# Pooled attention and a SiLU MLP on one core: q cast in its transfer, token parity on row halves, weights in full-partition loads, the first token tile in two column parts

## The chip, the core and the metric

The program runs on one NeuronCore of a Trainium2 chip. The core has TensorE (matmuls; "PE" in the profile, "PEld" for its weight loads), VectorE ("DVE"), ScalarE ("ACT"), GpSimd ("POOL") and SyncE ("SP"). Each engine works through its own instructions in order and waits on semaphores for others. Transfers between HBM and the on-chip memory SBUF are issued from SP's queue, POOL's queue or ACT's queue and run on 16 shared DMA engines; a transfer that changes the type (float32 to bf16) is issued from POOL here. Matmul results go to PSUM banks, from which VectorE and ScalarE copy them.

The metric is the time of one execution on the device in microseconds (us), the median of several runs.

## The reference

Keys and values are averaged over groups of 8 tokens, so each head attends from 576 queries to 72 pooled keys. The result, put back into token order, goes through a two-layer MLP with SiLU. All inputs and the output are float32.

```python
B, H, S, D = q.shape                                  # 8, 8, 576, 64
k_p = k.reshape(B, H, S // 8, 8, D).mean(axis=3)
v_p = v.reshape(B, H, S // 8, 8, D).mean(axis=3)
scores = (1 / np.sqrt(D)) * np.matmul(q, k_p.transpose(0, 1, 3, 2))
attn = np.exp(scores - scores.max(-1, keepdims=True))
attn = attn / (attn.sum(-1, keepdims=True) + 1e-09)
o = np.matmul(attn, v_p)                              # B, H, S, D
x = o.transpose(0, 2, 1, 3).reshape(B * S, H * D)     # 4608 x 512
h = x @ w_in                                          # 512 x 2048
out = (h * (1 / (1 + np.exp(-h)))) @ w_out            # 2048 x 512
```

## The kernel before

The 4608 tokens are 8 batches of 576 for the attention and 9 token tiles of 512 for the MLP. The attention of batch 0 stands ahead of everything. Then, for tile t, `up` (L299) makes 16 hidden groups of 128 features with 4 matmuls of 512 columns each, and ScalarE applies SiLU to each (L306); `down` (L319) makes 4 output blocks of 128 tokens with 16 matmuls each, VectorE copies a block out (L326) and SP stores it in two transfers of 64 rows (L329). While tile t runs, the attention of batch t+1 is woven in between its matmuls: `spread` takes a list of (step, work) pairs and issues each work item when the matmul count reaches its step. All instructions are placed by hand in this way (`manual_schedule`): an engine runs them in the order in which the code issues them.

Names that the prediction speaks of:

- `q_raw` (L98) is a batch of q in float32, loaded by two transfers of 64 partitions on SP's queue. POOL casts it to `q_bf` in four instructions (L109), TensorE transposes it to `qT_ps` in two groups of five and two of four (L121), VectorE copies to `qT` (L127). A token's number inside the batch is p * 9 + i; `qT` holds the tokens in the order (i, p), and the stores undo that order.
- K and V of batches 0 and 1 come "flat" (`load_kv_flat`, L182): K on partitions 0 to 63 and V on 64 to 127 of `kv_raw`. VectorE sums groups of 8 in a tree of additions (L145, L149), doubles the result (L196), TensorE transposes it (L206), and K goes to `kz`, V to `vT`, which is transposed back to `vp` (L226, L227). From batch 2 on, K and V come on 72 partitions each (`load_kv`, L137), are summed by the same tree, and K is transposed in four pieces (L165) and copied to `kz` (L173).
- `kz[n]` holds the keys of a pair of heads so that one half of the 128 rows is zero: a score matmul (L235) takes the 128 rows of two heads' queries and the key weights of one of them.
- `scores` makes two heads' scores for 288 tokens, with an exponential on ScalarE (`es`, L242). `values` makes the denominators (`den_ps`, L252), the numerators (`nu_ps`, L260), the reciprocal by a logarithm and an exponential on ScalarE (L268, L270) and the products into `xT` (L272). One pair of `scores` and one `values` is called a visit; a batch has four.
- `w_in_sb` is loaded by 16 casting transfers of 32 partitions on POOL's queue (L351), `w_out_sb` by 4 of 128 partitions behind them (L361). POOL's queue has eight completion semaphores: the ninth transfer is issued when the first has landed. POOL's casts of batch 1's q stand behind all of these.

Of the kernel before, what the change touches and what calls it, by code (L numbers as in the profile page):

```python
# [36 lines left out]
def kernel(  # L37
# [17 lines left out]
    NP = H // 2  # L55
# [3 lines left out]
    NT = NTOK // NTT  # L59

    QI = S // 64
    QC = (5, 4)

    KI = H * SP // 64
    S8 = 64 // H
    HS = S // 2
    score_scale = float(1.0 / (D ** 0.5) / POOL)
    assert NT == B + 1 and NP == KF and H == 8 and sum(QC) == QI == KI

    w_out_r = moe_w_out.rearrange("(kt kp) d -> kp kt d", kp=128)  # L70

    w_in_r = moe_w_in.rearrange("(g hh c dd) f -> hh c dd g f", g=2, hh=4, c=2)
    out_r = out.rearrange("(b p i) d -> b i p d", p=64, i=QI)

    singles = ctx.enter_context(tc.tile_pool(name="singles", bufs=1))
    big = ctx.enter_context(tc.tile_pool(name="big", bufs=2))
    mid = ctx.enter_context(tc.tile_pool(name="mid", bufs=2))
    psum = ctx.enter_context(
        tc.tile_pool(name="psum", bufs=1, space=bass.MemoryType.PSUM)
    )  # L80
    ctx.enter_context(tc.manual_schedule())


    ident = singles.tile([128, 128], BF16, name="ident")
    ones = singles.tile([SP, 32], BF16, name="ones")
    w_in_sb = singles.tile([128, KF, d_ff], BF16, name="w_in_sb")
# [3 lines left out]
    kz = [singles.tile([128, H, SP], BF16, name=f"kz{n}") for n in range(2)]  # L90
# [3 lines left out]
    def load_q(b):  # L94
        st = batches.setdefault(b, {})
        q_raw = big.tile([128, H // 2, QI * D], FP32, tag="q_raw", name="q_raw")
        for g in range(2):
# [4 lines left out]
        st["q_raw"] = q_raw  # L102

    def cast_q(b):
        st = batches[b]
        q_bf = big.tile([128, 2, QI, 2, D], BF16, tag="q_bf", bufs=1, name="q_bf")
        for a in range(2):
            for s in range(2):
                nc.gpsimd.tensor_copy(  # L109
                    out=q_bf[:, a, :, s, :],  # L110
                    in_=st["q_raw"][:, 2 * a + s, :].rearrange("q (i d) -> q i d", d=D),
                )
        st["q_bf"] = q_bf
        st["qT"] = mid.tile([128, NP, S], BF16, tag="qT", bufs=1, name="qT")

    def q_transpose(b, a, c):
        st = batches[b]
        i0, n = (0, QC[0]) if c == 0 else (QC[0], QC[1])
        qT_ps = psum.tile([128, n, 128], BF16, tag="nd", bufs=3, name="qT_ps")
        for i in range(n):  # L120
            nc.tensor.transpose(  # L121
                qT_ps[:, i, :],
                st["q_bf"][:, a, i0 + i, :, :].rearrange("q s d -> q (s d)"),
                ident,
            )
        dst = st["qT"].rearrange("d (g a) (i p) -> d a i g p", g=2, p=64)
        nc.vector.tensor_copy(  # L127
            out=dst[:, a, i0 : i0 + n],
            in_=qT_ps.rearrange("d i (g p) -> d i g p", g=2),
        )  # L130


    def load_kv(b):
        st = batches.setdefault(b, {})
        for name, src in (("k", k), ("v", v)):
            raw = big.tile([SP, H, POOL * D], FP32, tag=f"{name}_raw", bufs=1, name="raw")
            nc.sync.dma_start(  # L137
                out=raw, in_=src[b].rearrange("h (sp p) d -> sp h (p d)", p=POOL)
            )
            st[f"{name}_raw"] = raw  # L140

    def tree(dst, raw):
        w = POOL * D // 2
        while w > D:
            nc.vector.tensor_add(  # L145
                out=raw[:, :, :w], in0=raw[:, :, :w], in1=raw[:, :, w : 2 * w]
            )
            w //= 2
        nc.vector.tensor_add(out=dst, in0=raw[:, :, :D], in1=raw[:, :, D : 2 * D])  # L149

    def pool_k(b):
        st = batches[b]
        st["kp"] = mid.tile([SP, H, D], BF16, tag="kp", bufs=1, name="kp")
        tree(st["kp"], st["k_raw"])

    def pool_v(b):
        st = batches[b]
        st["vp"] = mid.tile([SP, H, D], BF16, tag="vp", name="vp")
        tree(st["vp"], st["v_raw"])

    def k_transpose(b):
        st = batches[b]
        kT_ps = psum.tile([128, NP, SP], BF16, tag="nd", bufs=3, name="kT_ps")
        for p in range(NP):
            nc.tensor.transpose(  # L165
                kT_ps[:, p, :],
                st["kp"][:, 2 * p : 2 * p + 2, :].rearrange("s h d -> s (h d)"),
                ident[:SP, :SP],
            )
        dst = kz[b % 2].rearrange("d (p s) k -> d s p k", s=2)  # L170
        for s in range(2):
            rows = slice(s * D, (s + 1) * D)
            nc.vector.tensor_copy(out=dst[rows, s], in_=kT_ps[rows])  # L173


    def load_kv_flat(b, parts):
        st = batches.setdefault(b, {})
        raw = big.tile([128, KI, POOL * D], FP32, tag="kv_raw", bufs=1, name="kv_raw")
        for i in range(parts):
            ii = slice(i * KI // parts, (i + 1) * KI // parts)  # L180
            for half, src in ((0, k), (64, v)):
                nc.sync.dma_start(  # L182
# [253 lines left out]
```

## Time and profile before

| | us |
|---|---|
| median of 3 runs | 351.69 |
| lowest and highest run | 351.60 and 650.59 |
| the profiled execution | 351.98 |
| its span in the profile | 350.2 |

The profiled execution is the one that all lines below come from; 1.8 us of it lie outside the span. In a line of the chain of waits stand the start, the length and what ran. In a line of the timeline stand start, length, engine, line of the code, operation, what it writes and reads, shape, count, and in brackets the idle time before it with what ended it. In a group line stand the busy time, the mean of one in ns, the idle time before such instructions and what ended it. In the windows stand the stretch, its length, the busy time (and count) of PE, PEld, DVE, ACT and POOL, the granted clock of TensorE, the mean busy share of the DMA engines and what they moved in GB/s. In the table of transfers stand the issuing queue, the count, the size of one as it lands in SBUF, and the median time to landing.

### The profile page before, as it was taken

To read this page: it belongs to the slowest core of one execution; us is meant where nothing else is said; L and a number is where in the kernel's file an instruction comes from. 1 tells how busy PE (TensorE), PEld (TensorE's weight loads), DVE (VectorE), ACT (ScalarE), POOL (GpSimd) and SP (SyncE) were. 2 spreads that over 40 slices of the span, in tenths; PEclk is the share of its full clock that TensorE was granted. 3 is DMA by queue.
4 is the path that set the end of the run, shared out by engine and by line. 5 is a ranking of instruction groups with operands and counts; after the bars stand their busy time and mean duration, and the time that the engine had idled before them with its cause. 6 is when DMAs were issued, how large, how long until landed. Compare 5 with 4: busy or idle time off the path is not lost.

```text
span 350.2 us, 4636 instructions
## 1 busy us (share of the span) xinstructions
PE 308.6 (88%) x1858; PEld 146.0 (42%) x1858; DVE 137.3 (39%) x204; ACT 177.3 (51%) x299; POOL 50.3 (14%) x61
## 2 busy tenths in 40 slices
PE   0336878499999999999999999999999999999994
PEld 0212334144544454445444544454445444444441
DVE  0641651033653456365546553754376231020011
ACT  1026628045675566555755665566566656604600
POOL 2731232000060006000500240033000000000000
PEclk9999989679999999999999999999999999999999
DMA  7999999612866296628653964496420021022022
GB/s 170 223 249 238 238 239 216 121 32 62 176 142 153 59 204 135 154 61 194 138 137 72 204 143 110 93 198 140 96 60 0 21 63 40 0 60 63 0 55 65
DMA packets 21221, 42.24 MB, mean 121 GB/s; under 512 B 2000, under 2 KB 4048, under 8 KB 21072
## 3 DMA queue, kind: packets, MB, share of 16 engines
q1 hardware_dynamic: 17808, 37.76, 47.2%
q0 software_dynamic: 3392, 4.20, 6.8%
q8 instruction: 14, 0.23, 0.3%
q14 instruction: 7, 0.06, 0.1%
HBM read 36.70 MB, written 9.44 MB: 132 GB/s over the span
## 4 chain that ended last, share of the span: by engine, by line
PE 74%; DMA 17%; ACT 4%; POOL 1%; issue 1%; SPq 0%; DVE 0%; POOLq 0%
PE o_ps L319 33%; PE hp_ps L299 32%; DMA w_in_sb<-in_moe_w_in_dram 8%; DMA w_out_sb<-in_moe_w_out_dram 7%; PE sc_ps L235 4%; ACT L277 2%; DMA q_raw<-in_q_dram 2%; PE nu_ps L260 2%; PE den_ps L252 2%; PE qT_ps L121 2%; ACT es L242 1%; ACT h_T L306 1%; POOL q_bf L109 1%; POOL w_out_sb L361 0%; PE kT_ps L165 0%
## 5 line engine op out<-in xcount | busy, mean ns | idle before, releaser
L319 PE MATMUL o_ps<-w_out_sb,h_T 128*128 128x512 bf16 x576 | 142.9, 385 | 6.1 <-DMA w_out_sb<-in_moe_w_out_dram 6.1
L299 PE MATMUL hp_ps<-xT,w_in_sb 128*128 128x512 bf16 x576 | 134.5, 385 | 0.0
L306 ACT ACTIVATE h_T<-hp_ps 128x512 bf16<-128x512 f32 x144 | 85.8, 597 | 70.5 <-PE hp_ps L299 70.4
L319 PEld LDWEIGHTS <-h_T 128*128 128x128 bf16 x576 | 56.2, 99 | 67.4 <-issue 15.8
L299 PEld LDWEIGHTS <-w_in_sb 128*128 128x128 bf16 x576 | 55.4, 99 | 61.6 <-issue 3.9
L272 DVE TENSOR_TENSOR xT<-nu_ps,rec 128x288 bf16<-128x288 f32 x64 | 26.3, 453 | 98.8 <-ACT rec L270 87.5
L109 POOL CAST q_bf<-q_raw 128x576 bf16<-128x576 f32 x32 | 37.0, 1196 | 167.0 <-PE qT_ps L121 118.6
L242 ACT ACTIVATE es<-sc_ps 72x576 bf16<-72x576 f32 x64 | 41.4, 647 | 28.4 <-PE sc_ps L235 28.2
L326 DVE COPY o_sb<-o_ps 128x512 f32<-128x512 f32 x36 | 24.8, 690 | 62.4 <-PE o_ps L319 62.4
L145 DVE TENSOR_TENSOR raw<-raw 72x2048 f32<-72x2048 f32 (+1 forms) x24 | 44.8, 1868 | 0.4
L235 PE MATMUL sc_ps<-qT,kz 128*72 128x288 bf16 x128 | 28.5, 307 | 7.7 <-ACT es L242 7.7
L268 ACT ACTIVATE lnd<-den_ps 128x288 f32<-128x288 f32 x32 | 13.1, 410 | 31.8 <-PE den_ps L252 31.8
L127 DVE COPY qT<-qT_ps 128x640 bf16<-128x640 bf16 (+1 forms) x32 | 14.5, 458 | 35.1 <-PE qT_ps L121 35.1
L121 PE MATMUL qT_ps<-ident,q_bf 128*128 128x128 bf16 x144 | 14.1, 233 | 12.8 <-POOL q_bf L109 12.7
L235 PEld LDWEIGHTS <-kz 128*72 128x72 bf16 x128 | 15.4, 122 | 21.5 <-issue 12.3
L121 PEld LDWEIGHTS <-q_bf 128*128 128x128 bf16 x144 | 11.2, 105 | 20.0 <-POOL q_bf L109 13.6
L260 PE MATMUL nu_ps<-es,vp 72*32 72x288 bf16 x256 | 14.8, 311 | 0.5 <-ACT lnd L268 0.5
L270 ACT ACTIVATE rec<-lnd 128x288 f32<-128x288 f32 x32 | 14.2, 445 | 1.0
L219 ACT COPY vT<-kvT_ps 64x160 bf16<-64x160 bf16 (+1 forms) x8 | 2.2, 274 | 21.5 <-DVE kz L216 21.3
L280 ACT ACT_TABLE_LOAD x9 | 11.5, 1283 | 0.2
L277 ACT ACT_TABLE_LOAD x8 | 10.3, 1283 | 0.9 <-PEq L420 0.7
L351 POOL DMA_DIRECT2D w_in_sb<-in_moe_w_in_dram x16 | 8.6, 544 | 13.8 <-DMA w_in_sb<-in_moe_w_in_dram 13.8
(26 smaller groups left out, 65.5 us busy)
## 6 DMA issues: line engine op xcount, KB each, us to landing
q_raw<-in_q_dram SPq DMA_DIRECT2D x16, 576.0 KB, 7.4
out_dram<-o_sb SPq DMA_DIRECT2D x72, 128.0 KB, 2.3
raw<-in_k_dram SPq DMA_DIRECT2D x6, 1152.0 KB
raw<-in_v_dram SPq DMA_DIRECT2D x6, 1152.0 KB
w_in_sb<-in_moe_w_in_dram POOLq DMA_DIRECT2D x16, 128.0 KB, 16.7
w_out_sb<-in_moe_w_out_dram POOLq DMA_DIRECT2D x4, 512.0 KB, 22.9
kv_raw<-in_k_dram SPq DMA_DIRECT2D x3, 384.0 KB, 10.6
kv_raw<-in_v_dram SPq DMA_DIRECT2D x3, 384.0 KB, 11.7
```

The source lines that it names most:

```text
L109: nc.gpsimd.tensor_copy(out=q_bf[:, a, :, s, :], in_=st["q_raw"][:, 2 * a + s, :].rearrange("q (i d) -> q i d", d=D),)
L121: nc.tensor.transpose(qT_ps[:, i, :], st["q_bf"][:, a, i0 + i, :, :].rearrange("q s d -> q (s d)"), ident,)
L145: nc.vector.tensor_add(out=raw[:, :, :w], in0=raw[:, :, :w], in1=raw[:, :, w : 2 * w])
L235: nc.tensor.matmul(sc_ps[:, s, :HS], lhsT=kz[b % 2][:, 2 * p + s, :], rhs=st["qT"][:, p, cols], start=True, stop=True,)
L242: nc.scalar.activation(es, sc_ps[:, :, :HS], func=AF.Exp, scale=score_scale)
L260: nc.tensor.matmul(nu_ps[32 * hh : 32 * (hh + 1), :HS], lhsT=st["vp"][:, 4 * g + hh, 32 * c : 32 * (c + 1)], rhs=es[hh // 2][:, hh % 2, :] ...
L272: nc.vector.tensor_mul(out=xT[:, 2 * g + c, cols], in0=nu[c][:, :HS], in1=rec)
L277: nc.scalar.preload_act_table_set("natural_log_exp_and_others")
L299: nc.tensor.matmul(hp_ps, lhsT=w_in_sb[:, kk, g * 128 : (g + 1) * 128], rhs=xT[:, kk, t * NTT : (t + 1) * NTT], start=(kk == 0), stop=(kk ...
L306: nc.scalar.activation(h, hp_ps, func=AF.Silu)
L319: nc.tensor.matmul(o_ps, lhsT=h_T[g][:, m * 128 : (m + 1) * 128], rhs=w_out_sb[:, g, :], start=(g == 0), stop=(g == KG - 1),)
L326: nc.vector.tensor_copy(out=o_sb, in_=o_ps)
```

## The change

The tokens of a batch are dealt differently. A token's number is now p * 18 + i with 32 values of p. q's transfer goes from POOL's queue and casts to bf16 on the way, with one row of 18 tokens per (head, p) on 128 partitions and two halves; `q_raw` and POOL's casts are gone. A transpose of 128 columns takes two neighbouring tokens (even and odd i), so `qT` holds the even tokens on rows 0 to 63 and the odd ones on rows 64 to 127. `kz[n]` gets a copy for each parity, with the other half of the rows zero; for this the pooled K is written twice (`kp` with a dimension of 2), transposed in 8 pieces instead of 4 and copied 64 x 576 instead of 64 x 288. The flat way of K and V is gone: all batches use 72 partitions, batch 0 in two halves of four heads each. The numerators take every second column of `vp`.

`w_in` comes in six transfers of 128 partitions (two rows of `w_in` per partition). q of batch 1 is issued between `w_in` and `w_out`, q of the later batches behind `w_out`. In batch 0 the order of the work is new, ScalarE copies `qT`, the last two visits take their reciprocal on VectorE, and eight matmuls on zeros stand at the head of TensorE's queue. PSUM is shared out differently for batch 0 (two score buffers, four of the others).

In tile 0, `up` runs all 16 groups on the first 288 columns and then on the other 224, with the work of batch 1 woven into the second part; `down` makes blocks 0 to 2 side by side, hidden group by hidden group, and then block 3. In the last tile the last block is made in two halves of 256 columns; the second half is copied by ScalarE and VectorE. A block is stored in four transfers of 32 rows.

```diff
-    def load_q(b):
+    def load_q(b, parts=1):
...
-            nc.sync.dma_start(
-                out=q_raw[64 * g : 64 * (g + 1), :, :],
-                in_=q[b, 4 * g : 4 * (g + 1)].rearrange("h (p i) d -> p h (i d)", i=QI),
-            )
...
-                nc.gpsimd.tensor_copy(
-                    out=q_bf[:, a, :, s, :],
-                    in_=st["q_raw"][:, 2 * a + s, :].rearrange("q (i d) -> q i d", d=D),
-                )
+            nc.gpsimd.dma_start(
+                out=q_bf[:, i * n : (i + 1) * n, :], in_=q_r[b][:, i * n : (i + 1) * n, :]
+            )
...
+    def load_one(b, name, parts=1):
...
+            nc.sync.dma_start(out=raw[:, hs, :], in_=src[:, hs, :])
...
+        tree([st["kp"][:, hs, u, :] for u in range(2)], st["k_raw"][:, hs, :])
...
-                lhsT=kz[b % 2][:, 2 * p + s, :],
-                rhs=st["qT"][:, p, cols],
+                lhsT=kz[b % 2][:, f, 2 * pr + u, :],
+                rhs=st["qT"][:, 2 * pr + u, :],
...
-                    lhsT=st["vp"][:, 4 * g + hh, 32 * c : 32 * (c + 1)],
+                    lhsT=st["vp"][:, 4 * g + hh, c::2],
...
+        if on_dve:
+            nc.vector.reciprocal(rec, den_ps[:, :HS])
...
+        for n in parts:
+            for g in range(KG):
...
+                    nc.tensor.matmul(
+                        hp_ps[:, :n],
+                        lhsT=w_in_sb[:, kk, g * 128 : (g + 1) * 128],
+                        rhs=xT[:, kk, t * NTT + n0 : t * NTT + n0 + n],
...
+            for cs in [slice(0, 256), slice(256, 512)] if final else [slice(0, 512)]:
+                for g in range(KG):
+                    for m, ps in zip(mm, o_ps):
...
+                    if cs.start:
+                        nc.scalar.copy(o_sb[:64, cs], ps[:64, cs])
+                        nc.vector.tensor_copy(out=o_sb[64:, cs], in_=ps[64:, cs])
...
-                nc.gpsimd.dma_start(
-                    out=w_in_sb[32 * hh : 32 * (hh + 1), c32::2, cs],
-                    in_=w_in_r[hh, c32][:, :, cs],
-                )
+        for c0, c1 in ((0, 512), (512, 1024), (1024, 2048)):
+            for g in range(2):
+                nc.gpsimd.dma_start(
+                    out=w_in_sb[:, 2 * g : 2 * g + 2, c0:c1], in_=w_in_r[g][:, :, c0:c1]
+                )
+        load_q(1)
...
+        h_T = up(t, f_up, (HS, NTT - HS) if t == 0 else (NTT,))
+        down(
+            t, h_T, f_down,
+            [(0, 1, 2), (3,)] if t == 0 else [(m,) for m in range(NTT // 128)],
+            last=t == NT - 1,
+        )
```

How the order of instructions moves is shown at three places. POOL's instructions from the start on, before (a row has the line, the operation, what it writes and reads, its shape and the count):

```order
L109 CAST q_bf<-q_raw 128x9x64 x4
L351 DMA w_in_sb<-in_moe_w_in_dram 32x2x1024 x16
L361 DMA w_out_sb<-in_moe_w_out_dram 128x4x512 x4
L109 CAST q_bf<-q_raw 128x9x64 x28
```

And now:

```order
L105 DMA q_bf<-in_q_dram 128x1152 x2
masks.py:197 MEMSET ident 128x128
masks.py:199 ISA
masks.py:199 AFFINE_SELECT ident<-ident 128x128
L324 DMA w_in_sb<-in_moe_w_in_dram 128x2x512 x4
L324 DMA w_in_sb<-in_moe_w_in_dram 128x2x1024 x2
L105 DMA q_bf<-in_q_dram 128x2x1152
L330 DMA w_out_sb<-in_moe_w_out_dram 128x4x512 x4
L105 DMA q_bf<-in_q_dram 128x2x1152 x6
```

POOL's queue now begins with q of batch 0 and has q of batch 1 ahead of `w_out`; the casts are gone. SP's queue, before, up to the stores of tile 0:

```order
L98 DMA q_raw<-in_q_dram 64x4x576 x2
L182 DMA kv_raw<-in_k_dram 64x1536
L182 DMA kv_raw<-in_v_dram 64x1536
L182 DMA kv_raw<-in_k_dram 64x1536
L182 DMA kv_raw<-in_v_dram 64x1536
L182 DMA kv_raw<-in_k_dram 64x1536
L182 DMA kv_raw<-in_v_dram 64x1536
L98 DMA q_raw<-in_q_dram 64x4x576 x2
L182 DMA kv_raw<-in_k_dram 64x4608
L182 DMA kv_raw<-in_v_dram 64x4608
L98 DMA q_raw<-in_q_dram 64x4x576 x2
L137 DMA raw<-in_k_dram 72x8x512
```

And now:

```order
L134 DMA raw<-in_k_dram 72x4x512 x2
L134 DMA raw<-in_v_dram 72x4x512 x2
L134 DMA raw<-in_k_dram 72x8x512
L134 DMA raw<-in_v_dram 72x8x512
L134 DMA raw<-in_k_dram 72x8x512
L134 DMA raw<-in_v_dram 72x8x512
L272 DMA out_dram<-o_sb 32x512 x16
```

SP's queue has only K and V ahead of the stores, and each load from the third on waits until VectorE has summed the batch before it out of the same buffer. TensorE's queue where `down` of tile 0 begins, before (the numbers tell tiles of one name apart: `o_ps_500` is the first output block, each `h_T` a hidden group, `kz1_75` the keys of batch 1):

```order
L319 LDWEIGHTS h_T_336
L319 MATMUL o_ps_500<-w_out_sb_72,h_T_336 128x512
L319 LDWEIGHTS h_T_343
L319 MATMUL o_ps_500<-w_out_sb_72,h_T_343 128x512
L235 LDWEIGHTS kz1_75
L235 MATMUL sc_ps_504<-qT_327,kz1_75 72x288
```

And now (`o_ps_564`, `565` and `566` are the blocks 0, 1 and 2):

```order
L288 LDWEIGHTS h_T_304
L288 MATMUL o_ps_564<-w_out_sb_70,h_T_304 128x512
L288 LDWEIGHTS h_T_304
L288 MATMUL o_ps_565<-w_out_sb_70,h_T_304 128x512
L288 LDWEIGHTS h_T_304
L288 MATMUL o_ps_566<-w_out_sb_70,h_T_304 128x512
```

Where one block walked through all hidden groups, and so through all of `w_out`, three blocks now take the same hidden group one after the other.

More of the change, by code (lines that the diff above doesn't have):

```diff
@@ L54 @@
     d_ff = moe_w_in.shape[1]
-    NP = H // 2
     KF = d_model // 128
@@ L168, in k_transpose @@
                 ident[:SP, :SP],
             )
[L170 to L182, printed above, removed]
-                    out=raw[half : half + 64, ii, :],
-                    in_=src[b].rearrange(
-                        "h (s i p) d -> (h s) i (p d)", s=S8, i=KI
-                    )[:, ii, :],
-                )
-        st["kv_raw"] = raw
```

350 lines of the change are left out of this document (166 added, 184 removed).

## The prediction

> **What bounds the kernel now.** I read the page's first block, then the chain of waits in order of time, then the windows of the DMA engines. First the page: span and TensorE.
>
> ```profile
> span 350.2 us, 4636 instructions
> PE 308.6 (88%) x1858; PEld 146.0 (42%) x1858; DVE 137.3 (39%) x204; ACT 177.3 (51%) x299; POOL 50.3 (14%) x61
> ```
>
> TensorE is busy 88% of the span, so at most 41.6 us could go without less matmul work. The chain (start, length, what) says where the rest sits.
>
> ```profile
> 1.57 7.26 DMA q_raw<-in_q_dram
> ...
> 12.08 9.61 DMA w_in_sb<-in_moe_w_in_dram
> ...
> 21.97 18.17 DMA w_in_sb<-in_moe_w_in_dram
> ...
> 43.73 25.22 DMA w_out_sb<-in_moe_w_out_dram
> ...
> 86.73 4.53 PE hp_ps L299 x21
> ...
> 120.64 4.53 PE hp_ps L299 x21
> ...
> 154.55 4.53 PE hp_ps L299 x21
> ```
>
> From 1.57 to 68.95 us (43.73 + 25.22) the chain is transfers almost alone. From 86.73 it is TensorE, and one token tile follows the other at 33.91 us (120.64 - 86.73 and 154.55 - 120.64). So the kernel has two stages: a start that waits for bytes up to 68.95, then 17.78 us of tile 0, then eight tiles bound by TensorE. The change can win in the first stage; in the second it can only add or remove TensorE work.
>
> How fast bytes come is read from the windows (stretch, its length, busy time of five engines, clock, DMA share, GB/s), and how many from the page's table of issues.
>
> ```profile
> 0.00:2.00 2.00, 0.00 (x0) 0.00 (x0) 0.00 (x0) 1.26 (x1) 1.39 (x9) 1.00 0.00 0
> ...
> 8.00:16.00 8.00, 2.78 (x21) 1.99 (x21) 3.81 (x9) 0.00 (x0) 6.81 (x12) 1.00 1.02 224
> 131.00:136.00 5.00, 5.00 (x29) 2.42 (x27) 4.43 (x3) 3.36 (x6) 4.38 (x3) 1.00 0.81 172
> ...
> 46.00:56.00 10.00, 10.00 (x60) 5.13 (x58) 3.58 (x8) 4.83 (x10) 2.71 (x5) 0.83 1.16 237
> 57.00:64.00 7.00, 4.05 (x23) 2.04 (x22) 0.00 (x0) 4.88 (x8) 0.00 (x0) 1.00 0.86 198
> q_raw<-in_q_dram SPq DMA_DIRECT2D x16, 576.0 KB, 7.4
> raw<-in_k_dram SPq DMA_DIRECT2D x6, 1152.0 KB
> w_in_sb<-in_moe_w_in_dram POOLq DMA_DIRECT2D x16, 128.0 KB, 16.7
> w_out_sb<-in_moe_w_out_dram POOLq DMA_DIRECT2D x4, 512.0 KB, 22.9
> ```
>
> Where transfers of both queues run, the share is 0.86 to 1.16: the DMA engines are full, and what counts is bytes. The table counts what lands: a q batch is two issues (1152 KB in float32), a K or V batch 1152 KB, the weights 16 x 128 + 4 x 512 = 4096 KB in bf16. Ahead of the last weights before go q of three batches, K and V of three, and the weights: 3456 + 6912 + 4096 = 14464 KB = 14.81 MB. Nothing moves in the first 2.0 us; from there to 68.95 it is 221 GB/s, between the rows' 198 and 237. The sum of bytes explains the landing.
>
> Two rows bound the kinds. Two 64-row halves side by side go at 224 GB/s (8 to 16 us); one 72-row K or V load alone goes at 172 (131 to 136 us).
>
> **The change part by part: the last weights.** q lands as bf16, so a batch costs 576 KB. q of batch 2 moves behind the weights in POOL's queue. Ahead of the last w_out piece then lie K and V of batches 0 to 2 (6912 KB), q of batches 0 and 1 (1152 KB) and the weights (4096 KB): 12160 KB = 12.45 MB. K of batch 2 is issued as soon as VectorE has summed K of batch 1, and V of batch 2 behind q's transposes of batch 1, whose q lies ahead of w_out; so I count both. At 221 GB/s this is 56.3 us, and the last piece lands at 58.3. The bounds: 12.45 MB at the slow mixed row of 198 gives 64.9; without V of batch 2 (11.27 MB) at 237 gives 49.6. I take the middle one, as it is the average that explained the landing before.
>
> [...]
>
> **Tile 0 behind the last weights.** Before, `down` finished one 128-token row block after the other, so all but a few of its 64 matmuls stood behind the last piece. Now three blocks go side by side, group by group.
>
> ```profile
> 60.96 1.02 PE L319 MATMUL o_ps<-w_out_sb,h_T 128*128 128x512 bf16 x4 [1.18 <-DMA w_out_sb<-in_moe_w_out_dram]
> ...
> 66.79 1.87 PE L319 MATMUL o_ps<-w_out_sb,h_T 128*128 128x512 bf16 x4 [4.56 <-DMA w_out_sb<-in_moe_w_out_dram]
> ...
> 173.78 0.31 PE L252 MATMUL den_ps<-es,ones 72*32 72x288 bf16 x4
> 173.91 0.42 PE L260 MATMUL nu_ps<-es,vp 72*32 72x288 bf16 x8
> 174.26 0.39 PE L319 MATMUL o_ps<-w_out_sb,h_T 128*128 128x512 bf16 x1
> 174.49 0.41 PE L235 MATMUL sc_ps<-qT,kz 128*72 128x288 bf16 x2
> 174.74 1.46 PE L319 MATMUL o_ps<-w_out_sb,h_T 128*128 128x512 bf16 x6
> ...
> L326 DVE COPY o_sb<-o_ps 128x512 f32<-128x512 f32 x36 | 24.8, 690 | 62.4 <-PE o_ps L319 62.4
> ```
>
> Behind the last piece stand 12 matmuls of the three blocks, 16 of the fourth, and of the attention of batch 1 two value groups and two score pairs. A warm matmul is 4.53/21 = 0.216 us (the row at 86.73). After a wait of 4.56 us four took 1.87 us, 0.47 each; after 1.18 us four took 1.02. The twelve follow a wait between these: half of them slow at 0.43, half at 0.216, 3.9 us (bounds 2.6 and 5.2). The fourth block reuses a bank of the first three, so TensorE waits for one VectorE copy (690 ns, the last row) and its semaphores, 1.0 us in all. Then 16 x 0.216 = 3.45, and by the starts above 2 x 0.48 + 2 x 0.25 = 1.46. Sum 9.8, against 17.78 before. Tile 1 starts at 58.3 + 9.8 = 68.1; that is 18.6 us earlier.
>
> [...]
>
> **What hides behind that.** The start of batch 0 is chained through VectorE and the K/V loads.
>
> ```profile
> 37.19 6.19 PE L299 MATMUL hp_ps<-xT,w_in_sb 128*128 128x512 bf16 x21
> L145 DVE TENSOR_TENSOR raw<-raw 72x2048 f32<-72x2048 f32 x12 | 28.4, 2370 | 0.0
> L145 DVE TENSOR_TENSOR raw<-raw 72x1024 f32<-72x1024 f32 x12 | 16.4, 1366 | 0.4
> L149 DVE TENSOR_TENSOR vp<-raw 72x512 bf16<-72x512 f32 x6 | 5.9, 976 | 0.2
> L149 DVE TENSOR_TENSOR kp<-raw 72x512 bf16<-72x512 f32 x6 | 4.1, 687 | 0.2
> 160.28 0.29 PE L165 MATMUL kT_ps<-ident,kp 72*128 72x72 bf16 x4
> 160.41 0.81 PE L299 MATMUL hp_ps<-xT,w_in_sb 128*128 128x512 bf16 x3
> ...
> PE qT_ps L121 <- POOL q_bf L109: 12.7, 2, 10.3
> ```
>
> K and V of batch 0 are 2304 KB = 2.36 MB: alone at 172 GB/s they land at 15.7 us, with half of the 237 GB/s at 21.9; I take 20. Half a V tree is (2.37 + 1.37 + 0.98)/2 = 2.4 us, and about 4 us of values, reciprocals and products follow: `up` starts near 27 instead of 37.19. w_in behind q of batch 0 (2.69 MB at half of 237) lands near 25, so it is no later than that. `up` is 64 x 0.216 = 13.8 us in two parts (the columns are the same, 288 + 224), about 3 us more for a slow clock at its start, and 1.3 us of transposes (18 of q, 8 of K); `down` with four attention visits is 13.8 + 4 x 0.98, and 1.0 for the copy. This ends at 63.8, 4.3 us ahead of 68.1: it is the cover of all startup edits (copies on ScalarE, split K and V, two reciprocals on VectorE), and the floor if the weights come sooner. TensorE waited for a POOL cast twice, in batch 0 and in tile 0 (the last row), and both waits end before the weights come: taking all 32 casts out is worth nothing more.
>
> **The steady tiles and the end.** K of a batch needs 8 transposes instead of 4: four took 0.13 us (160.28 to 160.41), so 0.13 more in six tiles, 0.8. K's last addition is done twice (0.69 more on VectorE), which ends about when TensorE reaches the transposes: 0 to 0.2 us a tile, taken as 0.5 in all. The 32-row stores double SP's issues, behind which only stores and the next K and V stand; nothing. The strided `vp` weights: nothing, as loads run ahead of matmuls (the rival below has the price). Steady: +1.3, bounds 0 and 2.5.
>
> ```profile
> 339.67 5.78 PE L319 MATMUL o_ps<-w_out_sb,h_T 128*128 128x512 bf16 x26
> ...
> 345.48 0.69 DVE L326 COPY o_sb<-o_ps 128x512 f32<-128x512 f32 x1 [2.76 <-PE o_ps L319]
> L260 PEld LDWEIGHTS <-vp 72*32 72x32 bf16 x256 | 7.1, 101 | 1.6 <-issue 0.8
> ```
>
> At the end the last copy is half as wide and shared by two engines, 0.69 to about 0.35: -0.3 (bounds -0.7 and +0.3, as four stores follow in place of two).
>
> **Sum.** 350.2 - 18.6 + 1.3 - 0.3 = 332.6 us of span. The profiled run took 351.98, 1.8 more than its span: 334.4 us. It was 0.3 above the median of 351.69, which I leave inside the range.
>
> **The rivals.** First: the weights land before the floor, and tile 1 starts at 63.8, 22.9 us earlier: 330. For it: casting loads that use all rows share the engines evenly at 46 to 56 us, where 237 GB/s flowed. Against it: K and V in 72 rows.
>
> Second: the engines run at the slow row throughout, the last piece lands at 64.9, tile 1 starts at 74.7: 12.0 us won, 341.0. For it: the row at 57 to 64 us is just this mix. [...]
>
> Third: the change doesn't bring the weights sooner. They land at 68.95 as now, because q now stands ahead of them in their own queue and the 72-row loads eat the saved bytes; only the side-by-side `down` stays. Tile 1 at 78.8, 8.0 us won: 345.0, within 2%. Against it: 2.36 MB fewer bytes.
>
> Fourth, on the other side: the strided `vp` weights (every second column) are no longer loaded ahead. Their row has 256 loads at 101 ns. Exposed in full they cost 25.9 us, 360.3 in all. It decides from 24.3/256 = 95 ns a load. Against it: eight matmuls with their loads now start within 0.35 us (173.91 to 174.26).
>
> **How the numbers follow.** The forecast has 0.50, its own range 331 to 338; the first rival 0.18, the second 0.18, the third 0.10, the fourth 0.04. About 2% is what a measurement can tell from no change, here 344.7 and 358.7. Faster: 0.50 + 0.18 + 0.16 of the second = 0.84; same: 0.02 + 0.10 = 0.12; slower 0.04. The range 328 to 343 leaves out the third and fourth (0.14) and 0.06 of the tails of the others.
>
> **What would show it.** The wait of `down` for w_out should end near 58 and tile 1's first `up` matmul stand near 68, with tiles 33.9 to 34.2 apart. `up` of tile 0 should begin near 27. If the period grows by more than 0.4 us, the strided loads or K's second addition cost; if the last w_out wait ends past 66, bytes were not saved or share badly; if no wait for w_out is left, tile 0 is bound by TensorE and the first rival holds.

## The result and the profile after

The changed kernel takes 331.53 us (median of 4 runs, 331.24 to 331.74) against 351.64 for the kernel before on the same chip: a ratio of 0.944, with a 95% interval of 0.9411 to 0.947. It is faster, inside the range, 2.9 us below the forecast of 334.4. Ratios leave out runs over 1.5% above the fastest of the same kernel: here one of 650.59 us of the kernel before, and below two of the four of `kv64` (338.75 and 339.07 us, beside 333.29 and 334.50). The profiled execution took 331.45 us, with a span of 329.7, against 350.2 before: 20.5 us less.

The head of the page (span, busy time, share, instructions):

```profile
span 329.7 us, 4895 instructions
PE 307.2 (93%) x1960; PEld 154.3 (47%) x1960; DVE 146.8 (45%) x216; ACT 177.6 (54%) x306; POOL 14.2 (4%) x25
```

TensorE is as busy as before (307.2 and 308.6 us), so what went is idle time: 41.6 us of it before, 22.5 now. The chain of waits up to tile 2 (start, length, what) says where it went and what bounds the start now:

```profile
1.24 8.57 DMA q_bf<-in_q_dram
9.85 1.14 PE qT_ps L116 x9
...
17.84 0.43 DVE vp L145
...
23.15 1.88 DVE rec L216
25.11 0.82 DVE xT L222 x2
25.94 1.88 DVE rec L216
27.91 0.83 DVE xT L222 x2
28.78 12.68 PE hp_ps L254 x85
...
65.84 4.53 PE hp_ps L254 x21
...
99.88 4.53 PE hp_ps L254 x21
```

Of the transfers that headed this chain up to 68.95, 8.57 us are left. Then VectorE leads (sums, two reciprocals, products), and from 28.78 on TensorE. Tile 1 starts at 65.84 instead of 86.73, 20.89 us earlier. The tiles are 34.04 apart instead of 33.91: 0.13 more, six times, 0.8. The last tile's `down` begins at 311.51 and the span ends at 329.7, 18.19 later; before it was 331.63 and 350.2, 18.57. So -20.89 + 0.78 - 0.38 = -20.5, the whole difference.

The list of what TensorE waited for (us in all, times, longest; this is its first row) has no row for `w_out` any more, and the view of the `w_out` transfers (the issue row: count, duration in ns, first and last start) says why:

```profile
PE qT_ps L116 <- DMA q_bf<-in_q_dram: 5.1, 1, 5.1
```

```profile
L330 POOL DMA_DIRECT2D w_out_sb<-in_moe_w_out_dram x4: 742/742/760, 12.0 to 20.8; - x4
...
DMA to landing us min/median/max: 30.6/33.6/34.0
```

The last piece was issued at 20.8 and landed 34.0 us later, at 54.8, where it was 68.95 before. Two totals of the transfers, from 2.00 to 68.95 us before and from 2.00 to 54.83 now, go with that:

```profile
DMA packets 6841, 14.83 MB, mean 222 GB/s; under 512 B 568, under 2 KB 2616, under 8 KB 6712
```

```profile
DMA packets 7591, 12.02 MB, mean 227 GB/s; under 512 B 300, under 2 KB 3372, under 8 KB 7588
```

The rate is nearly the same, and 2.8 MB fewer had gone by then: 1.8 of q, which lands in half the bytes, and 1.0 of V of batch 2, which now comes later. That is 14.1 of the 20.9 us. The other 6.8 lie behind that landing: from it to tile 1 it was 17.78 us, now it is 11.0, without a wait for weights. The timeline has the last piece wanted by the 37th matmul of `down`, the third of the six that begin here:

```profile
46.69 0.60 PE L288 MATMUL o_ps<-w_out_sb,h_T 128*128 128x512 bf16 x2
...
57.27 1.46 PE L288 MATMUL o_ps<-w_out_sb,h_T 128*128 128x512 bf16 x6
```

That is near 57.7, so the weights were there about 3 us ahead. This is the first rival's mechanism: tile 0 is bound by TensorE from the moment its `up` can start. V of batch 2, which the forecast put ahead of the last weights, was issued only at 49.70:

```profile
35.55 0.30 SPq L134 DMA_DIRECT2D raw<-in_k_dram  x1
49.70 0.30 SPq L134 DMA_DIRECT2D raw<-in_v_dram  x1
```

### The profile page after: what moved, and what is told of

Same layout as the page of the kernel before. It is cut to its first block, busy times and chain, and to the rows that moved or that the text cites. A ratio compares the mean times of both kernels' runs of the same rounds, so it can differ in the third digit from the quotient of the medians.

```text
span 329.7 us, 4895 instructions
## 1 busy us (share of the span) xinstructions
PE 307.2 (93%) x1960; PEld 154.3 (47%) x1960; DVE 146.8 (45%) x216; ACT 177.6 (54%) x306; POOL 14.2 (4%) x25
## 4 chain that ended last, share of the span: by engine, by line
PE 85%; ACT 6%; DVE 4%; DMA 3%; issue 1%; DVEq 0%; POOLq 0%
PE hp_ps L254 39%; PE o_ps L288 34%; PE sc_ps L182 4%; ACT L227 3%; DMA q_bf<-in_q_dram 3%; PE nu_ps L207 2%; PE qT_ps L116 2%; PE den_ps L199 2%; ACT es L189 2%; ACT h_T L260 1%; DVE raw L140 1%; DVE rec L216 1%; PE kT_ps L166 1%; DVE xT L222 1%; DMA out_dram<-o_sb 1%
## 5 line engine op out<-in xcount | busy, mean ns | idle before, releaser
L288 PE MATMUL o_ps<-w_out_sb,h_T 128*128 128x512 bf16 (+1 forms) x592 | 140.2, 374 | 0.6 <-DVE o_sb L300 0.5
L254 PE MATMUL hp_ps<-xT,w_in_sb 128*128 128x512 bf16 (+2 forms) x640 | 134.4, 363 | 2.7 <-DVE xT L222 2.7
L260 ACT ACTIVATE h_T<-hp_ps 128x512 bf16<-128x512 f32 (+2 forms) x160 | 88.7, 555 | 74.2 <-PE hp_ps L254 73.1
L254 PEld LDWEIGHTS <-w_in_sb 128*128 128x128 bf16 x640 | 62.0, 100 | 59.4 <-issue 2.9
L140 DVE TENSOR_TENSOR raw<-raw 72x1024 f32<-72x1024 f32 (+2 forms) x36 | 56.6, 1573 | 7.2 <-DMA raw<-in_k_dram 5.6
L300 DVE COPY o_sb<-o_ps 128x512 f32<-128x512 f32 (+1 forms) x36 | 24.4, 682 | 59.8 <-PE o_ps L288 59.7
L122 DVE COPY qT<-qT_ps 128x640 bf16<-128x640 bf16 (+1 forms) x28 | 12.8, 456 | 24.9 <-PE qT_ps L116 24.7
L105 POOL DMA_DIRECT2D q_bf<-in_q_dram x9 | 6.2, 691 | 157.7 <-PE qT_ps L116 131.0
L145 DVE TENSOR_TENSOR kp<-raw 72x512 bf16<-72x512 f32 (+1 forms) x18 | 10.5, 625 | 0.3
L199 PE MATMUL den_ps<-es,ones 72*32 72x288 bf16 x128 | 10.3, 312 | 0.0
```

The source lines that it names most:

```text
L140: nc.vector.tensor_add(out=raw[:, :, :w], in0=raw[:, :, :w], in1=raw[:, :, w : 2 * w])
L199: nc.tensor.matmul(den_ps[32 * hh : 32 * (hh + 1), :HS], lhsT=ones, rhs=es[hh // 2][:, hh % 2, :], start=True, stop=True,)
L254: nc.tensor.matmul(hp_ps[:, :n], lhsT=w_in_sb[:, kk, g * 128 : (g + 1) * 128], rhs=xT[:, kk, t * NTT + n0 : t * NTT + n0 + n], start=(kk = ...
L260: nc.scalar.activation(h_T[g][:, n0 : n0 + n], hp_ps[:, :n], func=AF.Silu)
L288: nc.tensor.matmul(ps[:, cs], lhsT=h_T[g][:, m * 128 : (m + 1) * 128], rhs=w_out_sb[:, g, cs], start=(g == 0), stop=(g == KG - 1),)
L300: nc.vector.tensor_copy(out=o_sb[:, cs], in_=ps[:, cs])
```

## The experiments

Theory after the result: the start is now a chain on VectorE and TensorE that ends in `up` at 28.78; the weights stand a few us behind it. Rivals: particular parts of the change carry the gain (column parts, side-by-side blocks, warm-up, q cast in its transfer, full-partition weight loads), or the weights are still the bound in disguise. Each kernel below is the changed kernel with one edit, unless it says otherwise. Ratios are to the kernel before on the same chip; the changed kernel's is 0.944, and it was not run again beside these. Two of these kernels with the same behaviour (`recip_act` and `late_v`) had tile 1 0.74 us apart, which is the measure for small differences of position.

| kernel | ratio, 95% interval | `up` starts | tile 1 starts | waits for `w_out` |
|---|---|---|---|---|
| changed | 0.944, 0.9411 to 0.947 | 28.78 | 65.84 | none |
| recip_act | 0.9513, 0.9482 to 0.9544 | 25.76 | 67.10 | 4.4 |
| block_order | 0.9642, 0.9574 to 0.971 | 28.81 | 68.20 | 2.6 |
| one_part | 0.9481, 0.9448 to 0.9514 | 28.83 | 65.14 | none |
| no_warm | one run, 330.46 us | 28.87 | 64.83 | none |
| one_pool | 0.9427, 0.9386 to 0.9468 | 27.98 | 65.51 | 0.7 |
| q_sp | 0.9579, 0.9518 to 0.9641 | 32.56 | 68.24 | none |
| kv64 | 0.9545, 0.9471 to 0.9618 | 31.87 | 68.98 | none |
| win32 | 0.9611, 0.9564 to 0.9658 | 34.13 | 70.94 | none |
| win2k | 0.9536, 0.9499 to 0.9572 | 31.73 | 68.31 | see text |
| late_v | 0.9529, 0.9483 to 0.9575 | 25.57 | 66.36 | 3.4 |
| combined | 0.9539, 0.9486 to 0.9592 | 25.92 | 68.04 | none |
| late_kv | 0.9498, 0.9463 to 0.9533 | 26.03 | 67.51 | none |

**recip_act: the two reciprocals back on ScalarE.**

```diff
-            values(0, g, 1, on_dve=True)
+            values(0, g, 1)
```

> Undoes one part: the last two visits of batch 0 take their reciprocal on ScalarE again (a logarithm and an exponential, 0.41 + 0.44 us) in place of VectorE (1.95 us each). Theory (the start of tile 0 is now set by batch 0's chain through VectorE, not by weights): the products end 2.5 to 3.3 us sooner, up of tile 0 starts at 25.5 to 26.3 us instead of 28.8, and 1 to 3 us of that reach the end, as the second half of w_in lands at 32 or 33: 328.5 to 330.5 us. Rival (the last weights still set tile 0, whatever up does): less than 0.5 us, 331 to 332.

`up` starts 3.0 us earlier, as forecast from two VectorE reciprocals of 1.95 us each. The gain expected from it did not come: tile 1 starts 1.3 us later. The timeline of the three waits (idle time and releaser in brackets):

```profile
48.75 0.59 PE L288 MATMUL o_ps<-w_out_sb,h_T 128*128 128x512 bf16 x2 [1.83 <-DMA w_out_sb<-in_moe_w_out_dram]
...
53.44 0.81 PE L288 MATMUL o_ps<-w_out_sb,h_T 128*128 128x512 bf16 x3 [0.86 <-DMA w_out_sb<-in_moe_w_out_dram]
...
58.96 1.02 PE L288 MATMUL o_ps<-w_out_sb,h_T 128*128 128x512 bf16 x4 [1.70 <-DMA w_out_sb<-in_moe_w_out_dram]
```

A faster start asks for the weights sooner, and the weights land later than in the changed kernel (58.9 for the last, where it was 54.8). K and V of batch 2 are issued when VectorE frees their buffers, so they came at 34.80 and 46.09 instead of 35.55 and 49.70. Whether they are what delays the weights was left to `late_v` and `late_kv`.

**block_order: tile 0's `down` one block after the other.**

```diff
-            [(0, 1, 2), (3,)] if t == 0 else [(m,) for m in range(NTT // 128)],
+            [(m,) for m in range(NTT // 128)],
```

> Undoes one part: down of tile 0 makes its four blocks one after the other. Theory (the last piece of w_out lands at 52 to 55 us, after it is wanted in this order at about 50.5, before it is wanted at 59.4 in the side-by-side order): a wait of 2 to 4 us for w_out comes back, 333 to 336 us. Rival (weights land ahead of either order): 331 to 332, and the 0.5 us wait for a copied-out bank goes.

```profile
50.41 1.02 PE L288 MATMUL o_ps<-w_out_sb,h_T 128*128 128x512 bf16 x4 [1.03 <-DMA w_out_sb<-in_moe_w_out_dram]
53.00 0.59 PE L288 MATMUL o_ps<-w_out_sb,h_T 128*128 128x512 bf16 x2 [1.57 <-DMA w_out_sb<-in_moe_w_out_dram]
```

In these timeline rows the first block asks for all of `w_out` within its 16 matmuls and waits 2.6 us; tile 1 is 2.4 us later. In this profiled run, of 333.82 us, the side-by-side order is worth that much, as the theory had it. The other three runs of `block_order`, which the ratio of 0.9642 counts too, took 338.11 to 338.81 us; they have no trace, so what that ratio holds beyond the 2.4 us is not known.

**one_part and no_warm: `up` of tile 0 on all 512 columns; no warm-up matmuls.**

```diff
-        h_T = up(t, f_up, (HS, NTT - HS) if t == 0 else (NTT,))
+        h_T = up(t, f_up)
...
-        n0 = KG * KF if t == 0 else 0
+        n0 = 0
```

```diff
-        warm_up(8)
```

> Undoes one part: up of tile 0 runs on all 512 columns at once, with batch 1's work woven in from its start. Theory: up began only after all products of batch 0 anyway, so the column parts won nothing by an earlier start; what they do is to push batch 1's transposes back behind the landing of its q (about 37 us), so without them TensorE waits 1 to 3 us for that q: 332.5 to 335. Rival (the parts are worth nothing or cost their 64 extra weight loads): 330.5 to 331.5.

> Leaves out the eight matmuls on zeros at TensorE's head. They end at 4.8 us and the next matmul comes at 9.8, so the clock should have fallen back by then. Theory: span 329.5 to 329.9 against 329.7. Rival (they keep the clock up for batch 0): the span grows by 1 to 3 us.

`one_part` starts `up` at the same time and reaches tile 1 0.7 us sooner: the first columns gain nothing, since their first matmul waits for the products of the second half too (the changed kernel's row at 27.91 ends just ahead of 28.78). The expected wait for q of batch 1 is there, but of 0.26 us only, and the ratio can't be told from the changed kernel's. `no_warm` starts `up` at the same time, and its first 85 matmuls take 11.59 us against 12.68. The same 85 took 11.31 to 12.74 in the other kernels that run `up` in two parts, and 12.62 in `late_kv`, which has no warm-up either. Behind the eight, in the changed kernel, TensorE is idle for 5.06 us; four score matmuls then take 1.12 us (at 11.83), as they do in `win32` (at 13.31), where the granted clock reads 0.53 from 8 to 14 us; the changed kernel's reads 1.00. So nothing shows that the eight matmuls buy anything, and whether they cost anything isn't told by one run.

**one_pool: one division of PSUM for the whole kernel.**

```diff
-    with tc.tile_pool(name="psum0", bufs=1, space=space) as psum0:
-        pools.update(psum=psum0, sc=2, nd=4)
+    psum = ctx.enter_context(tc.tile_pool(name="psum", bufs=1, space=space))
+    pools.update(psum=psum, mm=3, nd=3, sc=1)
+    if True:
```

> Changes one thing: batch 0 uses the PSUM shares of the rest of the program (one score buffer, three of the others, three for the MLP) in place of its own, so nothing has to be handed over before up. Theory (up's first part could start on the first 288 tokens but waits for the last products because its banks are those of batch 0): up starts 2 us or more before the last product, though batch 0 itself is up to 2 us slower with one score buffer: 329 to 333 us. Rival (the wait for the last products is one of data): up still starts right behind the last product and the time is 331.5 to 334.

```profile
27.98 3.30 PE L254 MATMUL hp_ps<-xT,w_in_sb 128*128 128x288 bf16 x13
```

`up` now begins straight behind the last numerators, while VectorE's last reciprocal and products still run (27.48 to 30.35 in its timeline). So in the changed kernel the wait of 2.7 us ahead of `up` is for PSUM: the banks of batch 0 must be free before the second division takes them. In batch 0 those products now end 1.6 us later (30.35 against 28.73), and TensorE waits for the exponentials between its score matmuls (0.73 us at 13.07 and at 16.23), as it has one score buffer. Tile 1 is 0.3 us earlier, which is less than the 0.74 of a repeat.

**q_sp: q in float32 through SP's queue, cast by POOL, as before the change.**

```diff
-            nc.gpsimd.dma_start(
-                out=q_bf[:, i * n : (i + 1) * n, :], in_=q_r[b][:, i * n : (i + 1) * n, :]
+            nc.sync.dma_start(
+                out=q_raw[:, i * n : (i + 1) * n, :], in_=q_r[b][:, i * n : (i + 1) * n, :]
...
+                nc.gpsimd.tensor_copy(out=q_bf[:, a, cs], in_=st["q_raw"][:, a, cs])
```

> Undoes one part: q comes in float32 on SP's queue, between K and V of batch 0, and POOL casts it as before; token order, weights and all else stay. Theory (the start is bound by bytes ahead of batch 0's chain, and the cast saves half of q's and 5 us of POOL): up of tile 0 starts 5 to 9 us later and most of it reaches the end, 336 to 341 us. Rival (q's way is hidden beside K and V): 331 to 333 us.

The waits of TensorE, by what it waited for:

```profile
PE qT_ps L125 <- POOL q_bf L116: 8.3, 2, 7.7
```

Tile 1 is 2.4 us later, between the two expectations: q's cast in the transfer, on POOL's queue, carries 2.4 of the 20.9 us. `up` starts 3.8 us later, for two reasons. q is ready later (TensorE waits 8.3 us for POOL where it waited 5.1 for the transfer) and VectorE's chain moves with it. Behind that V's second half, which now stands behind q in float32 on SP's queue, is not there yet (VectorE's timeline):

```profile
22.94 1.94 DVE L149 TENSOR_TENSOR raw<-raw 72x1024 f32<-72x1024 f32 x2 [1.35 <-DMA raw<-in_v_dram]
```

In the changed kernel this sum starts at 19.17. From `up` to tile 1 1.4 us come back, as the first 85 matmuls take 11.31 us against 12.68.

**kv64: K and V in 64 rows and 8 rows.**

```diff
-            nc.sync.dma_start(out=raw[:, hs, :], in_=src[:, hs, :])
+            for r in (slice(0, 64), slice(64, SP)):
+                nc.sync.dma_start(out=raw[r, hs, :], in_=src[r, hs, :])
```

> Changes one thing: each K and V load of 72 rows is issued as one of 64 rows and one of 8, so the larger one can use 16 engines. [...]

Windows of the DMA engines over one K load of a steady tile (stretch, length, five engines, clock, share, GB/s), kv64 first and then the changed kernel:

```profile
111.00:112.00 1.00, 1.00 (x10) 0.63 (x9) 0.00 (x0) 0.73 (x2) 0.00 (x0) 1.00 1.04 274
112.00:114.00 2.00, 2.00 (x14) 1.01 (x12) 0.49 (x1) 1.19 (x3) 0.00 (x0) 1.00 1.09 204
114.00:117.00 3.00, 3.00 (x16) 1.37 (x14) 2.92 (x3) 1.98 (x4) 0.72 (x1) 1.00 0.86 126
```

```profile
108.00:110.00 2.00, 2.00 (x14) 1.06 (x13) 0.49 (x1) 1.19 (x3) 0.00 (x0) 1.00 0.82 195
110.00:112.00 2.00, 2.00 (x14) 1.01 (x13) 1.11 (x2) 1.24 (x3) 0.72 (x1) 1.00 0.79 160
```

The share, a mean over 16 engines, rises from about 0.8 (0.82 and 0.79) to over 1.0 (1.04 and 1.09), and the peak to 274 GB/s, so the 64 rows fill the engines as the 72 did not. Why the 72-row load stays near 0.8 was not shown. But the load as a whole is no faster: the rate falls to 204 and then 126 GB/s (a row in which the next q begins too), and in both traces K's 1.18 MB have gone 8.4 us after the issue, at 108.55 in `kv64` and 105.40 in the changed kernel. In batch 0 VectorE's wait for V's second half grows from 0.90 to 2.28 us, and `up` starts 3.1 us later. Fuller engines for most of the rows didn't pay for a second transfer with the rest; the 72-row load stays the better of the two.

**win32 and win2k: `w_in` in 16 transfers of 32 partitions and 1024 columns; in four of 128 partitions and 1024 columns.**

```diff
-        for c0, c1 in ((0, 512), (512, 1024), (1024, 2048)):
-            for g in range(2):
+        for c0, c1 in ((0, 1024), (1024, 2048)):
+            for hh in range(4):
+                for g in range(2):
+                    ps = slice(32 * hh, 32 * (hh + 1))
...
-                    out=w_in_sb[:, 2 * g : 2 * g + 2, c0:c1], in_=w_in_r[g][:, :, c0:c1]
+                        out=w_in_sb[ps, 2 * g : 2 * g + 2, c0:c1],
+                        in_=w_in_r[g][ps, :, c0:c1],
```

```diff
-        for c0, c1 in ((0, 512), (512, 1024), (1024, 2048)):
+        for c0, c1 in ((0, 1024), (1024, 2048)):
```

> Undoes one part: w_in in 16 transfers of 32 partitions and 1024 columns in place of 6 over all 128 partitions. [...] Rival (full-partition loads are why the weights land sooner): w_in lands 5 us or more later and TensorE waits for it in up, 335 to 341 us.

> w_in in four transfers of 128 partitions and 1024 columns instead of six (the first columns in packets of 2 KB as in win32, but over all partitions). [...]

VectorE's sum of V's second half (timeline) in the changed kernel, win2k and win32:

```profile
19.17 1.94 DVE L140 TENSOR_TENSOR raw<-raw 72x1024 f32<-72x1024 f32 x2 [0.90 <-DMA raw<-in_v_dram]
```

```profile
22.11 1.95 DVE L140 TENSOR_TENSOR raw<-raw 72x1024 f32<-72x1024 f32 x2 [3.48 <-DMA raw<-in_v_dram]
```

```profile
24.51 1.94 DVE L140 TENSOR_TENSOR raw<-raw 72x1024 f32<-72x1024 f32 x2 [3.50 <-DMA raw<-in_v_dram]
```

V is summed 2.9 and 5.3 us later, and `up` starts 2.95 and 5.35 us later: V's landing sets `up`. The windows of 14 to 20 us, in the same order, tell two causes apart:

```profile
14.00:20.00 6.00, 4.60 (x28) 2.23 (x28) 4.45 (x8) 4.21 (x9) 1.48 (x2) 1.00 1.14 262
```

```profile
14.00:20.00 6.00, 4.23 (x27) 2.21 (x28) 3.54 (x7) 3.79 (x8) 0.74 (x1) 0.50 1.10 253
```

```profile
14.00:20.00 6.00, 4.30 (x27) 2.54 (x25) 4.04 (x8) 4.89 (x9) 2.67 (x5) 0.50 0.96 195
```

win2k moves about the same bytes per second, yet V is later: weights went ahead of V. The transfers by queue in the same 6 us show how, in the changed kernel and in win2k (q0 is POOL's queue and q1 SP's; packets, most of them rows of 1 or 2 KB, then MB and share of the engines):

```profile
q0 software_dynamic: 622, 0.76, 72.0%
q1 hardware_dynamic: 414, 0.81, 42.0%
```

```profile
q0 software_dynamic: 470, 0.91, 79.7%
q1 hardware_dynamic: 312, 0.61, 30.0%
```

For each packet of POOL's queue SP's had 0.67 and 0.66 of one. The ratio of the packets stays, and POOL's, now of 1.94 KB on average where they were of 1.22, take more of the bytes (0.91 MB where it was 0.76). How the engines choose between the queues was not shown beyond these counts. Another reason that comes to mind, that four transfers instead of six let POOL issue `w_out` at 6.54 instead of 12.02, is not it: by 21.2 us, when the last of V had moved in win2k, no packet of `w_out` had.

In win32 the rate itself falls to 195 GB/s, and V is another 2.4 us later; the form of the loads and their number (16; POOL issued two of q and six of these, and the ninth transfer waited 5.39 us, until q had landed) are not told apart. The profile names a `w_out` transfer as the releaser of `up` in win2k (2.7 us); the same 2.7 us stand there in the changed kernel behind the products, so no weight is missing. What was expected of win32 looked only at the weights; the last of `w_in` landed at 32.8 against 32.5, and nothing waited for it.

**late_v and combined.** `late_v` is `recip_act` with V of batch 2 written into `down` of tile 0. `combined` is `late_v` without the warm-up and with `up` of tile 0 in one part.

```diff
-                f_up.append((n0 + 51, lambda: load_one(a + 1, "v")))
+                fv = (f_down, 40) if t == 0 else (f_up, n0 + 51)
+                fv[0].append((fv[1], lambda: load_one(a + 1, "v")))
```

> As recip_act (reciprocals of batch 0 back on ScalarE), and V of batch 2 is issued in tile 0's down (step 40) instead of behind VectorE's sums in its up. Theory: V of batch 2, which recip_act issued at 46.1 us, shared the engines with the last w_out pieces and cost the 3 us that the earlier up had won. Then up starts near 25.8, the waits for w_out fall from 4.4 to under 1.5 us in all, and tile 1 starts between 62.8 and 64.5 us (span 326.5 to 328.5, ratio 0.937 to 0.943). Rival: the w_out pieces themselves, with K of batch 2, set the landing; the waits stay at 3 to 4.5 us and tile 1 starts at 66 to 67.2.

> late_v without the eight warm-up matmuls and with tile 0's up on all 512 columns at once. Theory: the three add up (no_warm had tile 1 1.0 us earlier, one_part 0.7), tile 1 at 61 to 63.2, span 324.5 to 327, ratio 0.933 to 0.940. Rival: the weights bind again as soon as up starts before 26 us, waits for w_out of 2 us or more return, and tile 1 stays at 64 to 65.5, the ratio at 0.941 to 0.946.

`late_v` says nothing about its theory: SP's queue was empty, so V was issued at 46.30 as soon as its buffer was free, wherever it stands among other engines' work. It serves as a repeat of `recip_act`. `combined` missed both ways. No wait for `w_out` is left; a new one stands ahead of it, in TensorE's timeline:

```profile
36.78 0.71 PE L116 MATMUL qT_ps<-ident,q_bf 128*128 128x128 bf16 x5 [4.54 <-DMA q_bf<-in_q_dram]
```

Without column parts the transposes of batch 1 come 64 matmuls sooner, and TensorE waits 4.5 us for q of batch 1, which stands behind `w_in`. So the column parts are a cover for q of batch 1, needed once `up` starts 3 us earlier.

**late_kv: `recip_act` without the warm-up, K and V of batch 2 through ScalarE's queue in tile 0's `down`.**

```diff
-            nc.sync.dma_start(out=raw[:, hs, :], in_=src[:, hs, :])
+            eng.dma_start(out=raw[:, hs, :], in_=src[:, hs, :])
...
+                if t == 0:
+                    f_down.append((2, lambda: load_one(a + 1, "k", eng=nc.scalar)))
+                    f_down.append((15, lambda: load_one(a + 1, "v", eng=nc.scalar)))
```

> As recip_act, without the eight warm-up matmuls, and in tile 0 the loads of K and V of batch 2 go through ScalarE's queue, behind the first and the fourth exponential of down (about 45.5 and 52 us), where SP's queue issued them at 34.8 and 46.1; late_v had left them there, since SP's queue was empty and issued V as soon as its buffer was free. Theory: those 2.3 MB, which shared the engines with w_out, are what turned recip_act's earlier up into waits for w_out. Then the last w_out piece lands before 53 us, the waits for w_out fall under 0.5 us, tile 1 starts between 61 and 63.5 us, span 324.5 to 327.5, ratio 0.932 to 0.940. Rival: w_out is held by its own queue (its packets cast one after the other) and not by K and V; then waits of 2 us or more stay, tile 1 starts at 65 to 67 and the ratio is 0.943 to 0.952. A third way: K of batch 2 comes too late for the first sum of tile 1 and its transposes wait; then tile 1 starts early but tile 2 does not follow 34.0 us behind it.

The view of the `w_out` transfers, first and last start at 12.1 and 21.1:

```profile
DMA to landing us min/median/max: 28.1/28.6/29.4
```

The last piece lands at 49.2 (21.1 + 28.1) instead of 58.9 in `recip_act`, and no wait for `w_out` is left. So K and V of batch 2 are what had turned the earlier start into waits: with K put off by 10 us and V by 6, the last weights come 9.7 us sooner, and the rival falls. Leaving out the warm-up isn't the reason, as that landing is at 56.0 in `no_warm`. Tile 1 still starts at 67.51. ScalarE's timeline shows the price of its queue, and TensorE's what followed:

```profile
45.20 4.93 ACTq L134 DMA_DIRECT2D raw<-in_k_dram  x1
50.18 0.65 ACT L189 ACTIVATE es<-sc_ps 72x576 bf16<-72x576 f32 x1 [3.79 <-issue]
```

```profile
50.88 0.30 PE L199 MATMUL den_ps<-es,ones 72*32 72x288 bf16 x2 [2.51 <-ACT es L189]
...
51.83 2.72 PE L288 MATMUL o_ps<-w_out_sb,h_T 128*128 128x512 bf16 x6
```

The issue of K held ScalarE for 4.93 us, TensorE waited 2.51 us for the exponential, and then ran slowly: six matmuls took 2.72 us, 1.46 elsewhere. `down` took 67.51 - 43.87 = 23.6 us, in the changed kernel 65.84 - 46.69 = 19.15. Without these 4.5 us tile 1 would start near 63.0, an estimate that no run here confirms. The third way did not happen: tile 2 follows 34.03 us behind.

No kernel of this study was shown to beat the changed one: `one_pool`'s interval contains 0.944. Nor do the parts that were undone one at a time make up the 20.9 us: q's cast has 2.4, the side-by-side blocks 2.4, the form of `w_in` 5.1. K and V in 72 rows in place of the flat form, and q of batch 2 behind the weights, were not undone.

## Why the prediction was right, and which of its steps failed

- **The start is bound by bytes up to 68.95, and the change wins there.** Right: all of the gain but 0.4 us of the end lies ahead of tile 1.
- **The last weights land at 58.3 and tile 0 waits for them.** This step failed. The last landed at 54.8, and nothing waited. The mis-sized term is V of batch 2, counted as ahead of them. Its buffer came free only behind V of batch 1, which VectorE summed from 45 us on, so it was issued at 49.70. The transfers by queue show what went in its place: SP's from 49.70 to 54.83, where only V of batch 2 was left, and POOL's from 2.00 to 54.83:

```profile
q1 hardware_dynamic: 82, 0.17, 9.6%
...
q0 software_dynamic: 4566, 5.96, 64.2%
```

Of V's 1.18 MB 0.17 had gone. POOL's queue had moved 0.59 MB more than the 5.37 of the weights and two batches of q; that is q of batch 2, which the sum put behind the weights. In all it was 12.02 MB at 227 GB/s in place of 12.45 at 221. By the prediction's own rate the bytes without V of batch 2 are 11.27 MB / 221 GB/s = 51.0, landing at 53.0; it had this sum as its lower bound, but with another rate, and took the middle one.
- **Tile 0 bound by TensorE would end at 63.8** (the cover, and the first rival). It did so at 65.84. `up` starts at 28.78 instead of 27; from there to tile 1 it is 37.06 us against the 36.8 that the prediction adds up. The 1.8 us are VectorE's: the prediction gave all that follows V's sum about 4 us and had no row for a reciprocal on VectorE. Each takes 1.95 us, and from the end of V's sum (21.14 + 0.42) to `up` it is 7.2 us. `recip_act` confirms it: there `up` starts 3.0 us sooner.
- **What 9.8 us behind the weights would have been** isn't tested, as no such wait was left.
- **Eight transposes cost 0.13 a tile:** right. **K's second addition costs 0.5 in all:** wrong, the period shows only the 0.13. **Strided `vp` weights cost nothing:** right; the fourth rival, whose loads would have added 25.9 us, isn't seen in the period.
- **Taking all POOL's casts out is worth nothing more.** Not borne out, as no weight was waited for: `q_sp`, which has the casts again and q in float32 on SP's queue, loses 2.4 us at tile 1; its two parts aren't told apart.
- **The end, -0.3:** -0.38.
- **The second and third rival** (slow rate, weights no sooner) fell with the landing: 54.8 is ahead of 64.9 and 68.95.

So the time came out 2.9 us below the forecast: 2.3 for tile 1 (68.1 against 65.84), 0.5 for K's addition, 0.1 at the end. The first rival's mechanism held at 0.18, where the forecast had 0.50; its 330 was 1.5 below the measured time. That the time still lies in the forecast's own range is luck as far as its mechanism goes: the cover of 63.8 happened to stand only 4.3 us below the forecast's start of tile 1, and VectorE made up 1.8 of them.

## What to carry to other kernels

When a transfer bound is removed, work out the chain behind it as carefully as the bytes: here weights and VectorE's chain end within a few us of each other, so that 3 us taken from one were lost to the other. For every load that is counted as competing, find what frees its buffer: here an empty queue issued V of batch 2 at that moment, wherever it stood in the program (49.70 us, 46.09 in `recip_act`, 46.30 in `late_v`), so a faster engine also brought it forward into the weights' way. Where two queues are busy together, count packets as well as bytes: here the longer packets of one queue (1.94 KB for 1.22) held up the other, whose V was summed 2.9 us later.

## What the runs showed of the hardware that was not expected

- A load of K issued from ScalarE's queue held it for 4.93 us; V's, 7 us later on the same queue, showed 0.33, and on SP's queue the same load of K took 0.30. It is not a matter of ScalarE alone: in the kernel before, SP's issue of V of batch 2 at 24.68 shows 13.39 us, and in `q_sp` its issue of q of batch 2 at 25.77 shows 5.48. Why these are so long isn't settled.
- The clock. In `late_kv` a wait of 2.51 us was followed by a granted clock of 0.50:

```profile
50.00:52.00 2.00, 1.12 (x14) 0.68 (x14) 0.00 (x0) 1.40 (x3) 0.00 (x0) 0.97 0.84 159
52.00:54.00 2.00, 2.00 (x6) 0.67 (x5) 0.82 (x2) 0.67 (x2) 0.00 (x0) 0.50 0.80 205
```

Between this wait and the first slow matmul stand matmuls of less than 1 us. In the kernel before, a wait of 4.56 us was followed by four matmuls in 1.87 us and a granted clock of 0.50 (66 to 74 us), and a wait of 1.18 us by four in 1.02. So not every wait between those two is without such a price; waits of 1.83 and 1.70 us in `recip_act` had none (two matmuls in 0.59 us and four in 1.02 behind them).

- The granted clock doesn't show every slow stretch. At the start of `up` in the changed kernel the windows of TensorE read:

```profile
30.00:32.00 2.00, 2.00 (x10) 1.00 1.13 254
...
34.00:36.00 2.00, 2.00 (x17) 1.00 0.83 211
```

Ten matmuls in 2 us and then seventeen, of the same 288 columns, both at a clock of 1.00. And in the rows of 14 to 20 us above TensorE was busy 4.60 us with 28 matmuls at 1.00 in the changed kernel, 4.23 us with 27 at 0.50 in win2k. So this row of a window doesn't tell by itself whether a stretch ran slowly.

- Sixteen casting loads of 32 partitions beside 72-row loads went with 195 GB/s in all, six of 128 partitions with 262, at shares of 0.96 and 1.14. In the kernel before, the same 32-partition form ran beside flat K and V loads, whose rows are up to 18 KB long (64 x 4608 in float32). From 26 to 36 us the transfers by queue read:

```profile
q1 hardware_dynamic: 178, 2.14, 92.7%
q0 software_dynamic: 170, 0.28, 15.1%
```

The packets of the two queues are nearly equal in number, and `w_in` in its 2 KB rows had 0.28 of 2.43 MB. So while these loads ran, the weights got a ninth of the bytes, a price of the flat form that a sum of bytes doesn't show.
